# Interleaving k and q heads over partitions, holding engines for the first groups' due steps, and whole Newton products in a fused attention and two-layer FFN kernel

## The chip, the cores and the metric

The kernel runs on one core of one Trainium2 chip. Its measure is the device time of one launch in microseconds, the median of several runs; smaller is better. The program is a single instruction stream per engine: TensorE (PE; its weight loads are listed apart as PEld), VectorE (DVE), ScalarE (ACT), GpSimd (POOL) and SyncE (SP), which issues the transfers.

## The reference, cut to what matters

```python
def _attn_ref(q, k, v):                      # 4 batches, 8 heads, 576 rows, 64 columns
    q_lm, k_lm = means of 18 neighbouring rows      # 32 landmarks per head
    A, Bm, C = sm(q, k_lm), sm(q_lm, k_lm), sm(q_lm, k)
    Z = Bm.transpose(0, 1, 3, 2) / (norm1(Bm) * norminf(Bm) + 1e-06)   # norms over the last two axes
    for _ in range(6):
        Z = 2 * Z - Z @ Bm @ Z
    return A @ Z @ C @ v
x = attention as (2304, 512)
h = x @ w_in;  x = (h * tanh(softplus(h))) @ w_out      # Mish layer, 512 -> 2048 -> 512
h = x @ w_in2; out = (h * sigmoid(h)) @ w_out2          # SiLU layer
```

The weights arrive as float64 and are turned into float32 on the chip. The attention is a Nyström approximation; its inner loop is a Newton iteration for the inverse of one 32x32 matrix per head.

## The kernel before, in words

**Work.** A "group" is four heads of one batch, so that four 32x32 landmark matrices fill 128 partitions; two groups make a batch, eight groups (0 to 7) make the attention. The FFN is split into units of 288 tokens and 128 hidden columns: six `h` matmuls (`h<-at,wp`), the Mish on ACT, a split of the result into a high and a low part (`g`), and twelve `y` matmuls (`y<-g,wo`). Layer 1 has 128 units, so 2304 matmuls of 128x288, which stand in batches' order: a batch needs both its groups, and the product of its matrix `ut` with a block of four decoded `w_in` tiles (`projection`, rows `t<-wa,ut`), from which come the `wp` tiles that the `h` matmuls take as weights. Layer 2 follows as seven-product blocks.

**Order.** The program is put in order while it is built: the class `Line` keeps a clock `now`, the time from which each engine is free, and a table of estimated costs. Every strand of work (a "chain") is a Python generator that yields the engine of its next step; `run` picks, among the chains that are due, the one of lowest rank (table `KINDS`: ranks 0 and 1 hold the FFN's gating, the projections `X` and the first two groups' chains `M` and `F`; ranks 2 and 3 hold the later groups and the decoding of weights). Each engine executes its instructions in the order so written. Where the plan has nothing for PE, it writes products of the identity (`y<-ident`, `h<-ident` and `t<-ident` without a second name), whose results nobody reads.

**Steps named below.** `Group.rows` loads k and q, 32 partitions per head. `transposed` and `scores` make the scores; `sums` makes the landmark sums (`lmk`, `lmq`) on DVE or POOL; in groups 2 and 3 they come from products with the constant `twice` instead. `newton` has six steps. In a step, `each` issues four 32x32 products, one per head (`t<-yu` or `h<-yu`), and DVE forms the next `yu`. The block-diagonal tile `bd` is built once per group on DVE and used for one last product (`bd,yu`). `decode` turns weights into float32: one ACT and three DVE instructions per tile (`wa`, `m`), for `wo` two more.

All engine instructions have line 226 (the helper `issue`), and all transfers line 237. In the changed program these are lines 257 and another; the names of tiles tell instructions apart.

Of the kernel before, what the change touches and what calls it, by code (L numbers as in the profile page):

```python
# [11 lines left out]
FP32 = mybir.dt.float32  # L12
# [47 lines left out]
def width(ap):  # L60
    return ap.size() // ap.shape[0]


class Line:
# [7 lines left out]
    WINDOW, ENOUGH = 4.096 / 1.2, 3060  # L72
    AGAIN = {"V": 0.12, "A": 0.12, "P": 0.1, "T": 0.0}
    FIXED = {"V": 0.07, "A": 0.1, "P": 0.05, "T": 0.0133}
    EACH = {"V": 1.04e-3, "A": 0.82e-3, "P": 2.29e-3, "T": 0.417e-3}

    def __init__(self, nc):
        self.nc = {"V": nc.vector, "A": nc.scalar, "P": nc.gpsimd, "T": nc.tensor}
        self.free = dict.fromkeys(["V", "A", "P", "T", "D", "W"], 0.0)
        self.now = 0.0  # L80
        self.free["D"] = 0.45
        self.end = 0.0
        self.last = set()
# [4 lines left out]
        self.small = False  # L88
        self.count = itertools.count()

    def cost(self, e, name, kw):
        src = kw.get("in_", kw.get("in0"))
        n = width(src if name == "tensor_reduce" else kw["out"])
        psum = src is not None and src.space == bass.MemoryType.PSUM
        more = 0.0
        if e == "T":
            tiled = kw["out"].shape[0] < 96 and "lhsT" in kw
            if tiled and (kw["out"].start_partition() or kw["lhsT"].start_partition()):
                return 0.027 * self.clock()
            n *= self.clock() * self.columns(kw)  # L100
        elif e == "A":
            more = -0.04 if psum else 0.0
            more += 0.14 if "accum_out" in kw else 0.09 if kw.get("func") == ACTF.Ln else 0.0
        elif e == "P" and name == "tensor_scalar":
            n *= 0.46
        elif e == "V" and name in ("copy", "tensor_copy", "tensor_scalar", "scaled"):
# [9 lines left out]
        return self.FIXED[e] + more + n * self.EACH[e]  # L116

    @staticmethod
    def span(ap):
# [71 lines left out]
    def issue(self, engines, name, kw, bias=0.0):  # L191
# [4 lines left out]
        e = min(engines, key=lambda e: start(e) + self.cost(e, name, kw) + (bias if e == "V" else 0.0))  # L196
        at = start(e)
        if e == "T":
            small = kw["out"].shape[0] < 96
            if self.small and not small:  # L200
                at = max(at, self.free["T"] + 0.055)
            self.small = small
        end = at + self.cost(e, name, kw)
# [25 lines left out]
    def transfer(self, engine, **kw):  # L229
        ap = kw["out"] if kw["out"].space == bass.MemoryType.SB else kw["in_"]  # L230
        start = max(self.now, self.free["D"], self.depend("D", "dma", kw))
        self.free["D"] = start + width(ap) * ap.shape[0] * 4 / 0.36e6
        end = self.free["D"] + 2.1
        self.end = max(self.end, end)
        self.last.add("D")
        self.record("D", kw, end)
        return engine.dma_start(**kw)  # L237

    def add(self, chain, rank, engine="W", ready=None):
        self.chains.append([self.now if ready is None else ready, rank, next(self.count), engine, chain])  # L240
        return self.chains[-1]

    def step(self, c):
        self.end = 0.0
        self.last = set()
        engine = next(c[4], "done")
        if engine == "done":
            self.chains.remove(c)
            return
        if not self.end:  # L250
# [10 lines left out]
    def run(self):  # L261
        while True:
            due = [c for c in self.chains if self.start_of(c) <= self.now]
            if not due:
                return
            self.step(min(due, key=lambda c: (KINDS[c[1]][0], c[2])))
# [81 lines left out]
def kernel(  # L348
# [648 lines left out]
    def heads(x, b, e):  # L997
        return x[b].rearrange("(i e) s d -> e i s d", e=GB)[e]

    class Group:  # L1000
# [7 lines left out]

        def load(self):
            kn = self.kn = qkv_p.tile([128, J, D], FP32, tag="kn", name="kn")  # L1010
            rows = [heads(x, self.b, self.hg).rearrange("i (l j) d -> i l (j d)", j=J) for x in (k, q)]
            self.rows(kn, rows[0])
            self.k_at = line.end
            if self.g == 1:
# [46 lines left out]
        def transposed(self, nm, src):  # L1061
# [6 lines left out]
            for j in range(0, J2, 3):  # L1068
# [30 lines left out]
        def main(self):  # L1099
# [28 lines left out]
            VAs.scaled(out=lmT[:, 0, :], in_=pl[0][:, 0, :], scalar1=1.0 / J)  # L1128
            VAs.scaled(out=lmT[:, 1, :], in_=pl[0][:, 1, :], scalar1=scale / J)
            Ring.give(pl)  # L1130
            self.lmT = lmT
            yield "W"
# [4 lines left out]
            for h in range(HG):  # L1137
# [56 lines left out]
            Ring.give(py)  # L1194
            yield "V"

            bd = self.bd = s_p.tile([128, HG, LM], FP32, tag="bd", name="bd")
            V.scalar_tensor_tensor(
                out=bd,
                in0=bn.rearrange("p (o l) -> p o l", o=1).to_broadcast([128, HG, LM]),  # L1200
                scalar=rc,
                in1=mask,
                op0=ALU.mult,
                op1=ALU.mult,
            )
            marks.add((g, "y"))
            yield "T"
            yield from until(marked((g, "u")))
# [3 lines left out]
        def each(out, lhsT, rhs, **kw):  # L1212

            for h in range(HG):
                r = slice(32 * h, 32 * h + 32)
                T.matmul(out=out[r], lhsT=lhsT[r], rhs=rhs[r], start=True, stop=True)

        def newton(self):

            yu, g = self.yu, self.g  # L1220
            for it in range(6):
# [15 lines left out]
            T.matmul(  # L1237
                out=pu[0][r], lhsT=yu[:, LM:], rhs=self.bd.rearrange("p h l -> p (h l)"), start=True, stop=True
            )
            yield "W"  # L1240
            VA.copy(out=ut_t[self.b][r].rearrange("p h l -> p (h l)"), in_=pu[0][r])
# [290 lines left out]
```

## Time and profile before

| | us |
|---|---|
| median of three runs | 858.45 (857.98 to 859.84) |
| span of the profiled execution, first to last instruction | 855.9 |
| PE busy | 824.3 (96%) |
| ACT busy | 450.6 |
| DVE busy | 515.6 |
| POOL busy | 288.1 |

The profile is one execution. The difference of 2.55 us between its span and the median of the runs is what lies around the first and last instruction, and the variation of runs. A float32 product that is not a transpose is listed as two matmul instructions, and a matmul's listed duration overlaps the next one's, so its price is read from start to start.

### The profile page before, as it was taken

The numbers are of one execution on the slowest core, as the hardware profiler recorded it, in microseconds if no ns is written. First come the engines' busy times: TensorE is split into PE (matmuls) and PEld (weight loads), VectorE is DVE, ScalarE is ACT, GpSimd is POOL, SyncE is SP. The second block draws the span as 40 slices with busy tenths as digits, with TensorE's granted clock in tenths as the row PEclk, the third lists the DMA queues.
The fourth block names the chain that finished last, engine by engine and source line by source line (L and its number), as shares of the span: only waits on it lengthen the run. The fifth ranks groups of instructions, "written<-read, shape, count | busy, mean of one in ns | idle before, by whom it ended". The sixth has DMA issues, their size and how long they took to land.

```text
span 855.9 us, 15972 instructions
## 1 busy us (share of the span) xinstructions
PE 824.3 (96%) x6084; PEld 726.1 (85%) x6084; DVE 515.6 (60%) x1030; ACT 450.6 (53%) x997; POOL 288.1 (34%) x331
## 2 busy tenths in 40 slices
PE   7999989899999999999999999999999999999996
PEld 5877767676899989989999898898898898998885
DVE  4976644453586958414516999767555567555542
ACT  5574776667555565433425755544544454544432
POOL 4241524342355555624323434311223221232210
PEclk9999999999999999999999999999999999999999
DMA  9874225200345554241125422101400000200002
GB/s 246 237 224 154 59 55 139 57 29 2 106 148 176 157 197 155 80 129 56 57 79 156 152 99 87 37 1 38 111 1 1 0 1 8 67 1 2 0 1 75
DMA packets 42254, 72.36 MB, mean 85 GB/s; under 512 B 5056, under 2 KB 31680, under 8 KB 42176
## 3 DMA queue, kind: packets, MB, share of 16 engines
q1 hardware_dynamic: 41600, 70.54, 27.1%
q8 instruction: 48, 0.79, 0.4%
q10 hardware_dynamic: 576, 0.79, 0.3%
q14 instruction: 30, 0.25, 0.1%
HBM read 57.15 MB, written 14.16 MB: 83 GB/s over the span
## 4 chain that ended last, share of the span: by engine, by line
PE 86%; ACT 7%; DMA 3%; issue 1%; DVE 1%; SPq 1%; POOL 0%; ACTq 0%; POOLq 0%; DVEq 0%
PE y L226 47%; PE h L226 31%; PE t L226 8%; ACT L226 3%; ACT z L226 1%; DMA wst<-in_moe_w_in_dram 1%; SPq L237 1%; DMA kn<-in_k_dram 1%; ACT g L226 1%; ACT ec L226 1%; DMA wst<-in_moe_w_out_dram 1%; DMA wst<-ys 0%; ACT at L226 0%; DMA out_dram<-ysb 0%; ACT wp L226 0%
## 5 line engine op out<-in xcount | busy, mean ns | idle before, releaser
L226 PE MATMUL y<-g,wo 128*128 128x288 f32 x1536 | 235.0, 301 | 1.4 <-POOL g L226 1.4
L226 PEld LDWEIGHTS y<-g,wo 128*128 128x128 f32 x1536 | 209.8, 188 | 15.3 <-issue 9.8
L226 PE MATMUL y<-wo,xg 128*128 128x512 f32 x693 | 179.8, 394 | 0.0
L226 POOL TENSOR_TENSOR g<-z,g 128x288 fp32r<-128x288 f32 x128 | 114.5, 905 | 174.3 <-ACT g L226 150.5
L226 PEld LDWEIGHTS y<-wo,xg 128*128 128x128 f32 x693 | 128.4, 188 | 20.9
L226 DVE TENSOR_TENSOR z<-h,z 128x384 f32<-128x384 f32 x164 | 89.4, 554 | 70.9 <-PE h L226 68.8
L226 PE MATMUL h<-at,wp 128*128 128x288 f32 x768 | 121.0, 302 | 5.8 <-ACT z L226 5.7
L226 PEld LDWEIGHTS h<-at,wp 128*128 128x128 f32 x768 | 106.3, 188 | 19.1 <-ACT z L226 8.8
L226 ACT ACTIVATE z<-h 128x288 f32<-128x288 f32 x128 | 51.6, 413 | 73.9 <-PE h L226 71.5
L226 ACT ACTIVATE z<-z 128x384 f32<-128x384 f32 x94 | 49.2, 525 | 34.3 <-DVE z L226 34.0
L226 POOL TENSOR_TENSOR wo<-m,wo 128x512 fp32r<-128x512 f32 x32 | 46.5, 1454 | 54.7 <-ACT wo L226 47.7
L226 DVE SCALAR_TENSOR_TENSOR m<-wst,m 128x512 int32<-128x512 int32 x64 | 61.9, 968 | 1.1
L226 PE MATMUL h<-xg,wp 128*128 128x384 f32 x288 | 58.0, 336 | 1.5 <-DVE z L226 1.5
L226 PE MATMUL h<-xg,wf 128*128 128x384 f32 x288 | 57.9, 336 | 0.4 <-DVE z L226 0.4
L226 ACT CAST g<-z 128x288 fp32r<-128x288 f32 x123 | 51.8, 435 | 7.4 <-PE y L226 6.2
L226 PEld LDWEIGHTS h<-xg,wp 128*128 128x128 f32 x288 | 51.3, 188 | 5.0 <-DVE z L226 1.9
L226 PEld LDWEIGHTS h<-xg,wf 128*128 128x128 f32 x288 | 51.2, 188 | 3.9 <-DVE z L226 0.9
L226 DVE TENSOR_TENSOR xg<-z,xg 128x384 fp32r<-128x384 f32 x73 | 41.4, 570 | 20.9 <-ACT xg L226 20.6
L226 POOL TENSOR_TENSOR wf<-m,wf 128x256 fp32r<-128x256 f32 x20 | 16.2, 809 | 96.8 <-ACT wf L226 96.8
L226 PE MATMUL y<-wo,wp 128*128 128x512 f32 x171 | 44.9, 394 | 0.0
L226 ACT ACT_TABLE_LOAD x31 | 39.8, 1283 | 1.7 <-PEq L1516 0.7
L226 DVE TENSOR_TENSOR wp<-t,wp 128x512 fp32r<-128x512 f32 x32 | 20.6, 685 | 30.5 <-ACT wp L226 30.4
(229 smaller groups left out, 1179.8 us busy)
## 6 DMA issues: line engine op xcount, KB each, us to landing
wst<-in_moe_w_out_dram SPq DMA_DIRECT2D x32, 512.0 KB, 5.8
wst<-in_moe_w_in_dram SPq DMA_DIRECT2D x28, 512.0 KB, 5.4
kn<-in_k_dram SPq DMA_DIRECT2D x32, 144.0 KB, 5.3
vn<-in_v_dram SPq DMA_DIRECT2D x8, 576.0 KB, 6.1
yh<-ysb SPq DMA_DIRECT2D x32, 144.0 KB, 1.9
ysb<-yh SPq DMA_DIRECT2D x32, 144.0 KB, 2.9
ys<-ysb SPq DMA_DIRECT2D x32, 144.0 KB, 2.0
qn<-in_q_dram SPq DMA_DIRECT2D x28, 144.0 KB, 3.6
```

The source lines that it names most:

```text
L226: r = getattr(self.nc[e], name)(**kw)
L237: return engine.dma_start(**kw)
```

## The change

Three edits and a new table of estimates. In `rows`, the four heads of k and q are spread over the partitions (partition 4l+h holds landmark l of head h) where each head had 32 neighbours; `transposed` and `main` undo it when they copy from PSUM. In `run`, an engine that a first-group chain or a projection will want within 0.4 us is not given to a chain of rank 2 or 3. In `newton`, groups 2 to 7 multiply by a block-diagonal tile in one product of 128x96, and DVE builds that tile anew for every step (`blocks`); the old `bd` is built after the six steps. The estimates get new numbers: POOL's cost per element, transfer rates, table loads of ACT's functions, and the switch of PE between 32-wide tiles and whole products.

```diff
-    EACH = {"V": 1.04e-3, "A": 0.82e-3, "P": 2.29e-3, "T": 0.417e-3}
+    EACH = {"V": 1.04e-3, "A": 0.82e-3, "P": 2.67e-3, "T": 0.417e-3}
+    TABLES = {ACTF.Exp: "exp", ACTF.Mish: "mish", ACTF.Silu: "silu"}
+    LOAD = 1.3
+    AHEAD = 0.4
...
@@ run @@
             due = [c for c in self.chains if self.start_of(c) <= self.now]
+            soon = {c[3] for c in self.chains if c[1] in "MFX" and not c[5] and self.now < c[0] <= self.now + self.AHEAD}
+            due = [c for c in due if KINDS[c[1]][0] < 2 or c[3] == "W" or c[3] not in soon]
...
@@ Group.load, Group.rows @@
-            rows = [heads(x, self.b, self.hg).rearrange("i (l j) d -> i l (j d)", j=J) for x in (k, q)]
+            rows = [heads(x, self.b, self.hg).rearrange("i (l j) d -> l i (j d)", j=J) for x in (k, q)]
...
-                line.transfer(nc.sync, out=to[32 * i:32 * i + 32].rearrange("p j d -> p (j d)"), in_=of[i])
+                line.transfer(nc.sync, out=to[i::HG].rearrange("l j d -> l (j d)"), in_=of[:, i])
...
@@ transposed @@
-                VA.copy(out=t[:, j:j + 3].rearrange("p j h l -> p j (h l)"), in_=pt[0])
+                VA.copy(out=t[:, j:j + 3], in_=pt[0].rearrange("p j (l h) -> p j h l", h=HG))
...
@@ newton @@
+        def blocks(self, y, by):
+
             V.scalar_tensor_tensor(
+                out=self.bd,
+                in0=y.rearrange("p (o l) -> p o l", o=1).to_broadcast([128, HG, LM]),
+                scalar=by,
                 in1=mask,
                 op0=ALU.mult,
                 op1=ALU.mult,
             )
...
+            whole = g > 1
             for it in range(6):
                 lo = 0 if it < 5 else LM
+                if whole:
+                    yield "V"
+                    self.blocks(yu[:, 0:LM], 1.0)
+                    yield "T"
                 yield from until(self.banks.ready)
                 pn = self.banks.take([128, LM + D], FP32)
-                self.each(pn[0][:, lo:], yu[:, 0:LM], yu[:, lo:])
+                if whole:
+                    T.matmul(out=pn[0][:, lo:], lhsT=bd, rhs=yu[:, lo:], start=True, stop=True)
+                else:
+                    self.each(pn[0][:, lo:], yu[:, 0:LM], yu[:, lo:])
...
+            yield "V"
+            self.blocks(self.bn, self.rc)
+            yield "T"
```

The order on PE around the first projection (`t<-wa,ut`), from the end of group 1's Newton steps (`h<-yu`, `h<-bd,yu`) on, before:

```order
L226 MATMUL h<-bd,yu 64x128
L226 MATMUL y<-ident 128x128 x6
L226 MATMUL t<-Tk,twice 128x128 x9
L226 MATMUL t<-Tq,twice 128x128 x9
L226 MATMUL y<-ident 128x128 x6
L226 MATMUL t<-wa,ut_141 32x512 x8
L226 MATMUL y<-ident 128x128 x14
L226 MATMUL t<-lmT 32x32 x4
L226 MATMUL y<-ident 128x128 x6
L226 MATMUL h<-at_637,wp 128x288 x2
```

and in the change:

```order
L257 MATMUL h<-bd,yu 64x128
L257 MATMUL t<-ident,kn 128x128 x3
L257 MATMUL t<-ident,qn 128x128 x3
L257 MATMUL y<-ident 128x128 x2
L257 MATMUL t<-ident,kn 128x128 x3
L257 MATMUL y<-ident 128x128 x2
L257 MATMUL t<-ident,qn 128x128 x3
L257 MATMUL y<-ident 128x128 x6
L257 MATMUL t<-wa,ut_141 32x512 x8
L257 MATMUL y<-ident 128x128 x20
L257 MATMUL t<-Tk,twice 128x128 x9
L257 MATMUL h<-at_644,wp 128x288 x2
```

The eighteen products with `twice`, which belong to group 2, stood ahead of the projection and now stand behind it, nine of them ahead of the first FFN matmul (`h<-at,wp`).

The order on DVE during group 1's Newton steps (`yu<-yu,h`; those of group 0 read `t`), with the decoding of weights (`wa`, `m`) between them, before:

```order
L226 SCALAR_TENSOR_TENSOR yu<-yu,h 128x96
L226 SCALAR_TENSOR_TENSOR yu<-yu,t 128x64
L226 SCALAR_TENSOR_TENSOR wa<-aw_145,wa 128x512 x2
L226 SCALAR_TENSOR_TENSOR yu<-yu,h 128x96
L226 TENSOR_SCALAR m<-m 128x512
L226 SCALAR_TENSOR_TENSOR wa<-aw_145,wa 128x512
L226 SCALAR_TENSOR_TENSOR m<-wst,m 128x512
L226 SCALAR_TENSOR_TENSOR yu<-yu,h 128x96
L226 TENSOR_SCALAR m<-m 128x512
L226 SCALAR_TENSOR_TENSOR m<-wst,m 128x512
L226 SCALAR_TENSOR_TENSOR yu<-yu,h 128x64
```

and in the change, from the same step of group 0 (`yu<-yu,t 128x64`) on:

```order
L257 SCALAR_TENSOR_TENSOR wa<-wst,wa 128x512
L257 SCALAR_TENSOR_TENSOR bd<-bn,rc,mask 128x128
L257 SCALAR_TENSOR_TENSOR yu<-yu,h 128x96
L257 TENSOR_SCALAR wa<-wa 128x512 x2
L257 SCALAR_TENSOR_TENSOR wa<-wst,wa 128x512
L257 SCALAR_TENSOR_TENSOR yu<-yu,h 128x96
L257 SCALAR_TENSOR_TENSOR wa<-aw_145,wa 128x512
L257 SCALAR_TENSOR_TENSOR wa<-wst,wa 128x512
L257 SCALAR_TENSOR_TENSOR yu<-yu,h 128x64
L257 SCALAR_TENSOR_TENSOR wa<-aw_145,wa 128x512
```

The decoding of `m` tiles has moved behind group 1's last step, and so has part of the decoding of `wa`.

The order on PE in a late group's Newton steps among the FFN's matmuls, before (group 6):

```order
L226 MATMUL t<-yu 32x96 x4
L226 MATMUL y<-g,wo 128x288 x2
L226 MATMUL t<-ident,kn 128x128 x3
L226 MATMUL y<-g,wo 128x288
L226 MATMUL t<-yu 32x96 x4
L226 MATMUL y<-g,wo 128x288 x3
```

and in the change (group 6):

```order
L257 MATMUL t<-yu,bd 128x96
L257 MATMUL y<-g,wo 128x288
L257 MATMUL t<-ident,qn 128x128 x3
L257 MATMUL y<-g,wo 128x288 x3
L257 MATMUL t<-lmT 32x32 x4
L257 MATMUL h<-at_1338,wp 128x288 x6
L257 MATMUL h<-at_2200,wp 128x288 x2
L257 MATMUL t<-yu,bd 128x96
```

Four 32x32 products have become one whole product, and more FFN matmuls stand between two steps. On DVE, group 2's steps read in the change:

```order
L257 SCALAR_TENSOR_TENSOR bd<-yu,mask 128x128
L257 TENSOR_SCALAR lmT<-t 128x128
L257 SCALAR_TENSOR_TENSOR m<-wst,m 128x512
L257 TENSOR_SCALAR m<-m 128x512
L257 SCALAR_TENSOR_TENSOR yu<-yu,t 128x96
L257 TENSOR_REDUCE nmb<-t 128x1
L257 SCALAR_TENSOR_TENSOR m<-wst,m 128x512
L257 SCALAR_TENSOR_TENSOR bd<-yu,mask 128x128
```

where there was a `yu` row alone; the `bd` rows are new, 36 in all.

## Rows read from the trace of the kernel before

**Rows 1.** Windows by stage: length, busy us per engine, granted clock, DMA share, GB/s.

```profile
0.00:50.50 50.50, 45.63 (x576) 36.19 (x577) 38.30 (x102) 26.84 (x67) 18.54 (x31) 1.00 0.91 251
...
83.10:223.70 140.60, 130.23 (x1452) 99.32 (x1451) 66.32 (x200) 97.74 (x201) 52.09 (x61) 1.00 0.21 57
```

**Rows 2.** PE's longest waits from 83.1 to 223.7 us: total, times, longest.

```profile
PE t L226 <- ACT ec L226: 5.8, 5, 1.5
PE h L226 <- ACT z L226: 3.0, 4, 1.0
```

**Rows 3.** PE's timeline once the attention is over: start, length, instruction, count.

```profile
223.68 6.75 PE L226 MATMUL y<-g,wo 128*128 128x288 f32 x48
230.27 4.20 PE L226 MATMUL h<-at,wp 128*128 128x288 f32 x30
```

**Rows 4.** PE's timeline in group 7's Newton steps.

```profile
214.75 0.37 PE L226 MATMUL t<-yu 32*32 32x96 f32 x8
215.05 1.06 PE L226 MATMUL y<-g,wo 128*128 128x288 f32 x6
216.04 0.37 PE L226 MATMUL t<-yu 32*32 32x96 f32 x8
```

**Rows 5.** PE's timeline: group 0's first k, group 1's first q.

```profile
5.65 0.87 PE L226 MATMUL t<-ident,kn 128*128 128x128 f32 x3 [1.47 <-DMA kn<-in_k_dram]
...
13.20 0.52 PE L226 MATMUL h<-ident,wp 128*128 128x128 f32 x3 [0.79 <-DMA wp<-in_q_dram]
```

**Rows 6.** Windows while k and q load, and while weights load.

```profile
3.00:13.00 10.00, 7.10 (x37) 5.75 (x35) 4.51 (x4) 3.25 (x7) 3.36 (x5) 1.00 1.03 231
...
48.00:54.00 6.00, 6.00 (x70) 4.79 (x62) 3.77 (x15) 4.80 (x10) 2.31 (x2) 1.00 1.02 409
```

**Rows 7.** SP's timeline: the issues of the first load.

```profile
0.74 1.78 SPq L237 DMA_DIRECT2D kn<-in_k_dram  x4
```

**Rows 8.** Timelines: group 1's `lmq` on POOL (first, last), its `lmk` on DVE.

```profile
13.22 1.41 POOL L226 TENSOR_TENSOR t<-wp 128x576 f32<-128x576 f32 x1 [1.29 <-DMA wp<-in_q_dram]
...
16.45 0.45 POOL L226 TENSOR_TENSOR lmq<-t,t 128x128 f32<-128x128 f32 x1
...
10.78 2.17 DVE L226 TENSOR_REDUCE lmk<-kn 128x64 f32<-128x1152 f32 x1 [2.79 <-DMA kn<-in_k_dram]
```

**Rows 9.** DVE's timeline: a decode instruction between group 1's Newton steps.

```profile
38.36 0.68 DVE L226 SCALAR_TENSOR_TENSOR wa<-aw,wa 128x512 int32<-128x512 int32 x1
```

**Rows 10.** PE's timeline from group 1's last product to the first FFN matmul.

```profile
41.15 0.43 PE L226 MATMUL h<-bd,yu 128*64 128x128 f32 x2
...
42.22 2.17 PE L226 MATMUL t<-Tk,twice 128*128 128x128 f32 x18
...
46.24 0.82 PE L226 MATMUL y<-ident 128*128 128x128 f32 x6
46.99 1.09 PE L226 MATMUL t<-wa,ut 64*32 64x512 f32 x16
...
50.52 0.51 PE L226 MATMUL h<-at,wp 128*128 128x288 f32 x2
```

**Rows 11.** PE's timeline around the second projection.

```profile
71.66 0.60 PE L226 MATMUL h<-ident 128*128 128x128 f32 x4
...
78.42 1.85 PE L226 MATMUL t<-wa,ut 64*32 64x512 f32 x16
...
83.11 0.50 PE L226 MATMUL h<-at,wp 128*128 128x288 f32 x2
```

**Rows 12.** All `bd` builds on DVE: min/median/max ns, first and last start.

```profile
L226 DVE SCALAR_TENSOR_TENSOR bd<-bn,rc,mask x8: 338/385/1240, 26.3 to 205.6; 128x128 f32<-128x128 f32 x8
```

**Rows 13.** Timelines of DVE and POOL at the longest `bd` build.

```profile
31.02 1.24 DVE L226 SCALAR_TENSOR_TENSOR bd<-bn,rc,mask 128x128 f32<-128x128 f32 x1
...
30.70 1.41 POOL L226 TENSOR_TENSOR at<-at,ar 128x576 f32<-128x576 f32 x1 [4.83 <-DVE ar L226]
```

**Rows 14.** The page's group of ACT's table loads: busy us, mean ns, idle before.

```profile
L226 ACT ACT_TABLE_LOAD x31 | 39.8, 1283 | 1.7 <-PEq L1516 0.7
```

More of the change, by code (lines that the diff above doesn't have):

```diff
@@ L74 @@
     FIXED = {"V": 0.07, "A": 0.1, "P": 0.05, "T": 0.0133}
-    EACH = {"V": 1.04e-3, "A": 0.82e-3, "P": 2.29e-3, "T": 0.417e-3}
+    EACH = {"V": 1.04e-3, "A": 0.82e-3, "P": 2.67e-3, "T": 0.417e-3}
+    TABLES = {ACTF.Exp: "exp", ACTF.Mish: "mish", ACTF.Silu: "silu"}
+    LOAD = 1.3
+    AHEAD = 0.4
+    TO_TILES, FROM_TILES, WEIGHTS = 0.092, 0.273, 0.107
     def __init__(self, nc):
@@ L88, in __init__ @@
         self.small = False
+        self.table = "exp"
         self.count = itertools.count()
@@ L96, in cost @@
         if e == "T":
-            tiled = kw["out"].shape[0] < 96 and "lhsT" in kw
-            if tiled and (kw["out"].start_partition() or kw["lhsT"].start_partition()):
-                return 0.027 * self.clock()
+            if "lhsT" not in kw:
+                return 0.002 + n * 2 * self.clock() * self.EACH["T"]
+            if kw["out"].shape[0] < 96:
+                at_once = 128 // kw["out"].shape[0] * (2 if kw["lhsT"].shape[0] == 64 else 1)
+                if kw["lhsT"].shape[0] == 128:
+                    at_once = 1
+                first = 0.0 if self.small else max(0.0, self.WEIGHTS - n * 2 * self.EACH["T"])
+                return first + n * 4 * self.clock() * self.EACH["T"] / at_once
+            if n == 512:
+                more = 0.005
+            if self.columns(kw) == 4:
+                n = max(n, 64)
             n *= self.clock() * self.columns(kw)
@@ L102, in cost @@
             more = -0.04 if psum else 0.0
-            more += 0.14 if "accum_out" in kw else 0.09 if kw.get("func") == ACTF.Ln else 0.0
+            more += 0.1 if "accum_out" in kw else 0.0
+            if name == "scaled":
+                more += 0.1
+            if src is not None and not psum and abs(src.ap[-1][0]) == 2:
+                more += 0.045
+            if self.table_of(name, kw) not in (None, self.table):
+                more += self.LOAD
         elif e == "P" and name == "tensor_scalar":
             n *= 0.46
+        elif e == "P" and "in1" in kw and not kw["in1"].ap[-1][0]:
+            n *= 0.73
         elif e == "V" and name in ("copy", "tensor_copy", "tensor_scalar", "scaled"):
@@ L116, in cost, with table_of @@
         return self.FIXED[e] + more + n * self.EACH[e]
+    def table_of(self, name, kw):
+        return self.TABLES.get(kw.get("func")) if name == "activation" else None
     @staticmethod
@@ L198, in issue @@
         if e == "T":
-            small = kw["out"].shape[0] < 96
+            small = kw["out"].shape[0] < 96 and "lhsT" in kw
             if self.small and not small:
-                at = max(at, self.free["T"] + 0.055)
+                at = max(at, self.free["T"] + self.FROM_TILES)
+            elif small and not self.small:
+                at = max(at, self.free["T"] + self.TO_TILES)
+        end = at + self.cost(e, name, kw)
+        if e == "T":
             self.small = small
-        end = at + self.cost(e, name, kw)
+        elif e == "A":
+            self.table = self.table_of(name, kw) or self.table
         if e == "T":
@@ L231, in transfer @@
         start = max(self.now, self.free["D"], self.depend("D", "dma", kw))
-        self.free["D"] = start + width(ap) * ap.shape[0] * 4 / 0.36e6
+        rate = 0.3e6 if ap.shape[0] == 96 else 0.4e6
+        self.free["D"] = start + width(ap) * ap.shape[0] * 4 / rate
         end = self.free["D"] + 2.1
@@ L239, in add @@
     def add(self, chain, rank, engine="W", ready=None):
-        self.chains.append([self.now if ready is None else ready, rank, next(self.count), engine, chain])
+        self.chains.append([self.now if ready is None else ready, rank, next(self.count), engine, chain, False])
         return self.chains[-1]
@@ L249, in step @@
             return
+        c[5] = not self.end
         if not self.end:
@@ L1127, in main @@
             lmT = s_p.tile([128, 2, 128], FP32, tag="lmT", name="lmT")
-            VAs.scaled(out=lmT[:, 0, :], in_=pl[0][:, 0, :], scalar1=1.0 / J)
-            VAs.scaled(out=lmT[:, 1, :], in_=pl[0][:, 1, :], scalar1=scale / J)
+            order = "p (h l) -> p h l" if g in SUMMED else "p (l h) -> p h l"
+            for i, by in enumerate((1.0 / J, scale / J)):
+                VAs.scaled(
+                    out=lmT[:, i, :].rearrange("p (h l) -> p h l", h=HG),
+                    in_=pl[0][:, i, :].rearrange(order, h=HG),
+                    scalar1=by,
+                )
             Ring.give(pl)
@@ L1195, in main @@
             yield "V"
[L1197 to L1205, printed above, removed]
+            self.bd = s_p.tile([128, HG, LM], FP32, tag="bd", name="bd")
             marks.add((g, "y"))
@@ L1237, in newton @@
             T.matmul(
-                out=pu[0][r], lhsT=yu[:, LM:], rhs=self.bd.rearrange("p h l -> p (h l)"), start=True, stop=True
+                out=pu[0][r], lhsT=yu[:, LM:], rhs=bd, start=True, stop=True
             )
```

6 lines of the change are left out of this document (added).

## Prediction

> **What bounds the kernel now.** I read the windows by stage first, then PE's waits, then PE's timeline at single places. PE is busy for 130.2 of 140.6 us while the later groups run beside the FFN, and ACT for 97.7, DVE for 66.3, POOL for 52.1 [rows 1]. PE's waits in that stage end on ACT, in the two largest groups 5.8 and 3.0 us, so about 9 us, or 6% [rows 2]. So from 83 us on PE's own work sets the pace, and an instruction taken off PE there is worth its full price, less those 6%. After the attention, 48 FFN matmuls take 230.27 - 223.68 = 6.59 us, 0.137 each [rows 3]. The first 50.5 us are another matter: PE looks busy for 45.6 of them [rows 1], but much of that is products of the identity that nobody reads. There the end is set by the chain from the landing of group 1's q to the first projection and the first FFN matmul at 50.52 us [rows 5, 10].
>
> So two things can shorten the span: an earlier first FFN matmul, if what follows moves with it, and less work on PE between 83 and 224 us.
>
> **The start, part by part.**
>
> Load. Group 0's first k is ready at 5.65 us, group 1's first q at 13.20, three loads later: 2.52 us per load of 4 x 144 KB [rows 5]. The core then moves 231 GB/s with its DMA engines full, against 409 when weights fill all 128 partitions [rows 6]. A load of 590 KB at 409 GB/s would take 1.44 us, but SP needs 1.78 us to issue its four transfers [rows 7], so the first load lands 1.1 us earlier and each further one 0.74: 3.3 us. No row shows a strided destination, so the ends are 0 (the rate is not the partitions' doing) and 4 x 1.08 = 4.3; I take 3.3, since 32 or 128 partitions is what sets the two windows apart.
>
> [...]
>
> Group 1's `lmq`. On POOL it runs from 13.22 to 16.90 us; a DVE reduction of the same size takes 2.17 [rows 8]. DVE has the `lmk` to do first, so of the 1.3 us about 0.6 are left; ends 0 and 1.3. On POOL nothing is queued behind it.
>
> Newton steps of group 1. By the order, the decode instructions between the last three steps are five of 0.68 us and two of 0.42 before, three and two in the change; an instruction of 0.68 stands in the row [rows 9]. With one or two more ahead of these, 1.5 us; ends 0 and 3.
>
> `twice`. From group 1's last product at 41.15 us to the projection at 46.99 pass 5.84 us, of which 4.02 are the eighteen products with `twice` [rows 10]. They go. What is late next is the decoding that was put off: seven DVE rows, four of them 0.68, one `bd` of 0.34 [rows 12] and two shorter, less their overlap 3.4 us from the last step, some 3.3 from the last product with the hand-over. Gain 2.5, ends 1 and 4. Nine `twice` products now stand between projection and first FFN matmul, which took 3.53 us [rows 10]; I charge 1 us, at most 2.0.
>
> Sum: 3.3 + 0.6 + 1.5 + 2.5 - 1 = 7 us, between -1 and 12.6. The first FFN matmul would start near 43.5 us.
>
> Then the FFN runs out of `wp` after 72 matmuls, before as in the change: PE idles with identity products from 71.66 us, the second projection starts at 78.42, the FFN goes on at 83.11 [rows 11]. That projection stands 31.4 us behind the first one. It waits for four decoded tiles, which ACT and DVE handle between Mish, table loads and group 2's chain; their transfers run from 48 to 54 us [rows 6], long before. By the order these instructions stand in the same places relative to the first projection, so I keep the 31.4 us and the 7 us carry over.
>
> **Newton on PE.** Six FFN matmuls and one step of four 32x32 products repeat every 216.04 - 214.75 = 1.29 us [rows 4]; six matmuls at 0.137 are 0.82, so a step costs 0.47, though only 0.30 pass from its start to the next matmul's. The rest is lost at the change between tiles and whole products. A whole float32 product of 128 columns takes 4.02 / 18 = 0.22 us [rows 10]. With 96 columns that would be 0.17 if columns alone counted (lower end); the upper end is 0.43, the listed length of `bd,yu` [rows 10]. I take 0.22, because a single product also loads its own weights. Outside the idle stretches stand 31 steps before (one of group 2, thirty of groups 3 to 7) and 33 in the change, as fewer of group 2's fall into the pause: 31 x 0.47 = 14.6 against 33 x 0.22 = 7.3. Less the 6% of waits this saves 7 us; with 0.17 it is 9, with 0.43 nothing.
>
> [...]
>
> **What is added elsewhere.** 36 `bd` builds on DVE, 0.34 to 1.24 us [rows 12], are 12 us or more; DVE is idle for 74 of 140.6 us in that stage [rows 1], so the time is covered. They lengthen each Newton step, so attention ends later in the FFN: the first projections of batches 1, 2 and 3 stand behind 234, 516 and 760 FFN matmuls (before 212, 436, 594), and the batches begin at 288, 576, 864. The margins are 54, 60 and 104 matmuls, 7.4 to 14 us at 0.137; nothing is charged. The copies that undo the interleaving read with a stride; ACT is idle for 43 us of the stage, so nothing again, though a copy twice as long would show in the waits on ACT. ACT has 27 table loads where it had 31, 5.1 us at 1.28 [rows 14]; this could shorten the waits on ACT by up to that, and I count none. SP issues its transfers as before but for one `w_in` tile that goes ahead of group 3's k. The second layer's instructions stay, so its time stays.
>
> **The sum.** 7 + 7 = 14 us. The profiled span of 855.9 us becomes 841.9; with the 2.5 us that the median has above it, 844.4. I forecast 844.
>
> **Rivals.**
>
> A. One of the two savings doesn't arrive. Either the second projection is tied to something else than the first (all seven microseconds go into a longer pause at 72 matmuls; for it: ACT is the busy engine there), or a single whole product costs near 0.43 us. 858.45 - 7 = 851.
>
> B. Neither arrives: the loads stay at 231 GB/s, the decoding that was put off eats what `twice` gave up, and whole products cost as much as tiles. 858. Against it: two unrelated places must fail.
>
> C. Slower. Each whole product waits in PE's queue for a `bd` that DVE builds one step earlier, and behind it wait the FFN matmuls. The place is the 36 builds. POOL works 37% of that stage [rows 1], and a `bd` that met a POOL instruction took 1.24 us in place of 0.34 and ended when that had ended [rows 13]: 0.9 us. With 24 of 36 so caught, 21.6 us against the 14 saved: 866. It decides from 16 on (16 x 0.9 = 14.4). For it: a decode instruction ahead of the `bd` on DVE adds another 0.68. Against it: between two steps stand mostly ten FFN matmuls or more, 1.4 us, and a `bd` and a `yu` need 0.6.
>
> D. More: the start gains its upper end, whole products cost 0.17 and fewer table loads shorten ACT's waits: 858.45 - 12.6 - 9 - 5 = 832 at most.
>
> **How the numbers follow.** Forecast (838 to 850) 0.50, A 0.23, B 0.07, C 0.12, D (under 838) 0.08. A measurement of this kernel tells about 0.2% (1.7 us) from no change. Faster by more: 0.50 + 0.23 + 0.08 = 0.81; within: 0.07; slower: 0.12. The range 833 to 857 holds the forecast, A and most of D, and leaves out C and most of B, some 0.2.
>
> **What would show it.** Right, if group 1's first q is transposed near 10 us and the window over the loads shows over 300 GB/s; if the first FFN matmul starts near 43.5 us and the second projection 31 us after the first; if a whole product adds about 0.22 us between FFN matmuls; and if the stage after the attention keeps 0.137 us per matmul. Wrong, if PE waits on DVE's `bd` ahead of these products, if the pause at 72 matmuls grows by as much as the start shrank, or if PE's waits on ACT exceed 9 us.

## The result, and the profile after

| us | median of the runs | first FFN matmul | behind 74 FFN matmuls | from there to 800 | from 800 to the end |
|---|---|---|---|---|---|
| before | 858.42 | 50.5 | 83.9 | 167.7 | 604.3 |
| change | 848.38 (846.67 to 850.29) | 50.9 | 84.3 | 157.7 | 604.9 |

The change is faster: ratio 0.988, interval 0.987 to 0.990, 10.0 us, where 14 were forecast. The profiled span is 846.9 us in place of 855.9. The columns behind the median are starts of FFN matmuls in the two traces; 74 is just behind the pause, in which the FFN has no `wp` left after 72 matmuls and PE writes products of the identity; by the 800th the attention is all but over. I call these two the marks. The start gained nothing, and the whole gain lies between the marks.

Windows of before over that stretch (length, busy us of PE, PEld, DVE, ACT, POOL, clock, DMA share, GB/s):

```profile
83.90:251.60 167.70, 157.33 (x1664) 125.57 (x1664) 85.65 (x223) 113.24 (x237) 66.17 (x75) 1.00 0.26 76
```

Windows of the change over the start (beside [rows 1]), the same stretch, the load, and three short ones:

```profile
0.00:50.95 50.95, 40.59 (x525) 30.87 (x525) 36.85 (x101) 25.68 (x62) 12.67 (x25) 0.97 0.75 234
...
84.30:242.00 157.70, 151.13 (x1480) 130.25 (x1479) 89.48 (x257) 101.05 (x220) 59.32 (x71) 0.98 0.19 56
...
3.00:8.00 5.00, 2.61 (x18) 2.03 (x17) 2.33 (x2) 0.96 (x2) 0.11 (x1) 1.00 0.74 230
...
11.60:15.00 3.40, 3.12 (x16) 2.75 (x15) 3.09 (x3) 1.80 (x5) 0.00 (x0) 0.50 0.94 238
...
90.10:93.50 3.40, 3.40 (x17) 3.40 (x16) 0.36 (x4) 2.28 (x7) 1.56 (x2) 0.50 0.00 0
107.10:110.60 3.50, 2.97 (x14) 2.95 (x15) 1.16 (x6) 1.60 (x4) 1.16 (x1) 0.51 0.00 0
```

PE is busy for 6.2 us less and idle for 6.6 us in place of 10.4. In the three short stretches its clock is halved (0.50, 0.50 and 0.51); in the trace of before the clock is full (1.00) from 11 to 853 us. The loads still move 230 GB/s, but now at a DMA share of 0.74, where [rows 6] had 1.03.

PE's longest waits in that stretch of the change, beside [rows 2]:

```profile
PE h L257 <- ACT z L257: 2.5, 4, 0.8
PE t L257 <- DVE yu L257: 1.9, 2, 1.2
PE t L257 <- ACT ec L257: 1.4, 2, 0.8
```

SP's timeline of the change, the first two loads, beside [rows 7]:

```profile
0.74 2.46 SPq L269 DMA_DIRECT2D kn<-in_k_dram  x4
3.24 2.50 SPq L269 DMA_DIRECT2D qn<-in_q_dram  x4
```

PE's timeline of the change, beside [rows 5, 10, 11], and whole products of late groups beside [rows 4]:

```profile
5.31 0.52 PE L257 MATMUL t<-ident,kn 128*128 128x128 f32 x3 [1.13 <-DMA kn<-in_k_dram]
...
12.95 0.87 PE L257 MATMUL h<-ident,wp 128*128 128x128 f32 x3 [0.28 <-DMA wp<-in_q_dram]
...
41.30 0.40 PE L257 MATMUL h<-bd,yu 128*64 128x128 f32 x2 [0.95 <-DVE bd L257]
...
45.37 1.47 PE L257 MATMUL t<-wa,ut 64*32 64x512 f32 x16 [0.87 <-ACT Tk L257]
46.77 2.40 PE L257 MATMUL y<-ident 128*128 128x128 f32 x20
49.01 2.18 PE L257 MATMUL t<-Tk,twice 128*128 128x128 f32 x18
50.95 0.51 PE L257 MATMUL h<-at,wp 128*128 128x288 f32 x2
...
78.86 1.09 PE L257 MATMUL t<-wa,ut 64*32 64x512 f32 x16
...
197.33 0.35 PE L257 MATMUL t<-yu,bd 128*128 128x96 f32 x2
197.47 0.77 PE L257 MATMUL h<-at,wp 128*128 128x288 f32 x4
...
221.99 0.36 PE L257 MATMUL t<-yu,bd 128*128 128x96 f32 x2
222.13 1.31 PE L257 MATMUL h<-at,wp 128*128 128x288 f32 x8
223.28 0.95 PE L257 MATMUL y<-g,wo 128*128 128x288 f32 x6
224.07 0.35 PE L257 MATMUL t<-yu,bd 128*128 128x96 f32 x2
```

One load takes SP 2.5 us, and group 1's first q comes three of those behind the first k (12.95 - 5.31 = 3 x 2.55). That SP now sets this pace shows in the time from a transfer's issue to its landing. For group 1's q, the last of the four loads, its median (the last number) is 5.1 us in before, where SP starts a load every 1.85 us and one is ready every 2.52, and 2.6 in the change, as for the first loads, where it starts one every 2.53 and one is ready every 2.55:

```profile
wp<-in_q_dram SPq DMA_DIRECT2D x4, 144.0 KB, 5.1
```

```profile
wp<-in_q_dram SPq DMA_DIRECT2D x4, 144.0 KB, 2.6
```

The first projection stands 1.6 us earlier than before, the second one 33.5 us behind it in place of 31.4. A whole product is followed by the next FFN matmul after 0.14 us, and from one whole product over fourteen FFN matmuls to the next pass 224.07 - 221.99 = 2.08 us.

SP's longer issues also put off what SP issues behind the loads. A decode instruction of ACT waits 1.82 us for its weights, `ec` stands behind it in ACT's queue, and PE waits 1.36 us for `ec`. ACT's timeline of the change, then PE's:

```profile
20.90 0.66 ACT L257 ACTIVATE wa<-wst 128x512 f32<-128x512 f32 x1 [1.82 <-DMA wst<-in_moe_w_in_dram]
```

```profile
22.31 0.44 PE L257 MATMUL y<-ident 128*128 128x128 f32 x2 [1.36 <-ACT ec L257]
```

Behind the 800th matmul PE's largest wait in the change is a new one, 2.6 us. PE's timeline there, then ACT's:

```profile
330.17 1.35 PE L257 MATMUL h<-at,wp 128*128 128x288 f32 x8 [2.61 <-ACT z L257]
```

```profile
326.03 0.41 ACT L257 ACTIVATE z<-h 128x288 f32<-128x288 f32 x1 [0.23 <-PE h L257]
328.82 0.66 ACT L257 ACTIVATE wi<-wst 128x512 f32<-128x512 f32 x1 [2.38 <-DMA wst<-in_moe_w_in_dram]
329.39 0.42 ACT L257 CAST g<-z 128x288 fp32r<-128x288 f32 x1
329.71 0.41 ACT L257 ACTIVATE z<-h 128x288 f32<-128x288 f32 x1
```

A decode instruction waits 2.38 us for its weights, and the Mish behind it in ACT's queue, for which PE waits 2.61 us, has to wait too.

### The profile page after: what moved, and what is told of

It is laid out like the page before. It is cut to its first block, busy times and chain, and to the rows that moved or that the text cites. A ratio compares the mean times of both kernels' runs of the same rounds, so it can differ in the third digit from the quotient of the medians.

```text
span 846.9 us, 15538 instructions
## 1 busy us (share of the span) xinstructions
PE 815.8 (96%) x5866; PEld 729.2 (86%) x5866; DVE 523.8 (62%) x1082; ACT 446.2 (53%) x983; POOL 277.2 (33%) x322
## 4 chain that ended last, share of the span: by engine, by line
PE 86%; DVE 5%; DMA 3%; ACT 2%; SPq 2%; issue 2%; POOL 0%; ACTq 0%; DVEq 0%; POOLq 0%
PE y L257 48%; PE h L257 30%; PE t L257 8%; SPq L269 2%; DMA wst<-in_moe_w_in_dram 1%; DVE m L257 1%; DMA out_dram<-ysb 1%; ACT z L257 1%; DVE bd L257 1%; DVE wa L257 0%; DVE z L257 0%; DVE wp L257 0%; ACT wp L257 0%; DVE yu L257 0%; ACT g L257 0%
## 5 line engine op out<-in xcount | busy, mean ns | idle before, releaser
L257 PEld LDWEIGHTS y<-g,wo 128*128 128x128 f32 x1536 | 211.1, 190 | 13.3 <-issue 10.9
L257 DVE TENSOR_TENSOR z<-h,z 128x384 f32<-128x384 f32 x161 | 87.9, 555 | 70.2 <-PE h L257 68.3
L257 POOL TENSOR_TENSOR wo<-m,wo 128x512 fp32r<-128x512 f32 x31 | 44.7, 1444 | 53.5 <-ACT wo L257 48.4
L257 DVE SCALAR_TENSOR_TENSOR m<-wst,m 128x512 int32<-128x512 int32 x64 | 55.2, 870 | 0.4
L257 PEld LDWEIGHTS h<-xg,wf 128*128 128x128 f32 x288 | 51.2, 188 | 3.9 <-ACT z L257 0.9
L257 PEld LDWEIGHTS h<-xg,wp 128*128 128x128 f32 x288 | 51.2, 188 | 3.7 <-DVE z L257 0.6
L257 ACT CAST g<-z 128x288 fp32r<-128x288 f32 x118 | 49.5, 436 | 7.9 <-PE y L257 6.5
L257 POOL TENSOR_TENSOR wf<-m,wf 128x256 fp32r<-128x256 f32 x17 | 12.6, 742 | 83.9 <-ACT wf L257 83.9
L257 ACT CAST xg<-z 128x384 fp32r<-128x384 f32 x74 | 38.0, 513 | 1.6
L257 PEld LDWEIGHTS y<-wo,wp 128*128 128x128 f32 x171 | 31.7, 188 | 5.2
```

The costliest lines, as they stand in the source:

```text
L257: r = getattr(self.nc[e], name)(**kw)
```

## The experiments

All times are medians, all ratios against the kernel before, whose runs beside these had medians of 858.2 to 858.6 us. The columns are as above; they are of the one profiled execution, which took 2.1 us more than the median in d_estimates, 3.1 less in e_one_block, and lies between these in the others.

| kernel | us | ratio, interval | first FFN matmul | behind 74 | 74 to 800 | 800 to end |
|---|---|---|---|---|---|---|
| c_tiled | 846.12 | 0.986 (0.984 to 0.988) | 49.9 | 81.1 | 160.2 | 603.1 |
| c_block | 847.60 | 0.987 (0.984 to 0.989) | 49.6 | 83.0 | 154.8 | 608.0 |
| c_no_hold | 857.70 | 0.999 (0.997 to 1.000) | 56.5 | 84.1 | 165.6 | 606.9 |
| c_two_queues | 847.36 | 0.986 (0.984 to 0.988) | 50.4 | 83.7 | 154.9 | 607.2 |
| d_one_issue | 845.44 | 0.984 (0.982 to 0.986) | 46.2 | 79.5 | 157.8 | 606.5 |
| d_estimates | 851.47 | 0.991 (0.990 to 0.993) | 57.0 | 87.9 | 159.6 | 604.3 |
| d_hold | 864.52 | 1.007 (1.006 to 1.009) | 53.4 | 91.0 | 165.4 | 608.2 |
| d_old_estimates | 871.70 | 1.015 (1.013 to 1.018) | 50.2 | 88.1 | 167.2 | 615.4 |
| e_one_from3 | 837.04 | 0.975 (0.973 to 0.976) | 47.4 | 78.6 | 154.7 | 601.6 |
| e_one_tiled | 843.40 | 0.982 (0.981 to 0.984) | 47.7 | 78.9 | 160.0 | 602.3 |
| e_one_block | 877.11 | 1.021 (1.019 to 1.023) | 69.6 | 102.9 | 162.8 | 606.5 |
| e_whole | 865.80 | 1.008 (1.006 to 1.010) | 51.2 | 84.0 | 166.0 | 612.5 |

My first theory was that of the prediction with its start taken out: the whole products are the gain. The rivals were the hold, and the interleaved rows.

**c_tiled.** The change with tiles in every step.

```diff
-            whole = g > 1
+            whole = False
```

> The changed kernel, but all groups' Newton steps as four 32x32 products again (the interleaving, the hold and the new estimates stay). Theory 1, the gain of 10 us is PE time saved by whole products: 36 steps at about 0.25 us more each, so about 857 to 860 us, and the first FFN matmul at 51 us as in the change. Theory 2, the gain comes from the new order (hold and estimates) and the products' price is hidden: 850 us or less.

It was not slower, 846.1, and theory 1 fell. What the whole products take off PE is there: against c_block, whose order is that of the change and whose clock was full between the marks, the tiles add 4.0 us in the 33 steps themselves and 3.2 us in the FFN matmuls, 7.2 in all or 0.22 per step. Most of the 3.2 us stands just ahead of a step: from start to start such an FFN matmul takes 0.23 us in c_tiled, and 0.14 in c_block ahead of a whole product. But with tiles PE's idle time there is 3.7 us in place of 6.6, and the FFN goes on 1.9 us earlier than in c_block, 3.2 earlier than in the change. PE's timeline of c_tiled:

```profile
215.51 0.37 PE L257 MATMUL t<-yu 32*32 32x96 f32 x8
215.81 1.06 PE L257 MATMUL h<-at,wp 128*128 128x288 f32 x6
216.80 0.31 PE L257 MATMUL t<-yu 32*32 32x64 f32 x8
```

Six matmuls and a step take 1.29 us, as in [rows 4]; in the change four matmuls follow a whole product after 0.14 us.

**c_block.** The change with contiguous rows, as before, and the copies from PSUM that belong to them.

```diff
-                line.transfer(nc.sync, out=to[i::HG].rearrange("l j d -> l (j d)"), in_=of[:, i])
+                line.transfer(nc.sync, out=to[32 * i:32 * i + 32].rearrange("p j d -> p (j d)"), in_=of[i])
```

> The changed kernel with each head's k and q in 32 neighbouring partitions again. Theory 1, SP's issue of a strided transfer (0.64 us against 0.46) has become the limit of the first loads, so that the interleaving gains nothing there: issues 0.46 us apart, group 1's first q transposed at about 13 us as in both kernels, total within 2 us of 848.4. Theory 3, spreading shortens the loads' path: 3 us slower than 848.4, and the first q later than in the change.

With four transfers per load the interleaving makes no difference that the medians show (0.8 us, within the spread of either). At the start it costs: c_block's first FFN matmul comes 1.3 us earlier. SP issues the first `w_in` weights at 9.72 us in place of 12.03, ACT doesn't wait for them, and PE doesn't wait for `ec`. ACT's timeline of c_block:

```profile
19.23 0.68 ACT L257 ACTIVATE wa<-wst 128x512 f32<-128x512 f32 x1
```

The order on PE is that of the change, row for row, and the stretch from 74 to 800 takes 154.8 us in place of 157.7, with no half clock in it: so the two half-clock stretches cost the change 2.9 us there. c_block had its own elsewhere, of 6.8 us each from 8.0 and from 325.4 us on.

**c_no_hold.** The change without the hold.

```diff
-            due = [c for c in due if KINDS[c[1]][0] < 2 or c[3] == "W" or c[3] not in soon]
```

> The changed kernel without the hold of engines for the first groups' due steps. Theory 1 (whole products are the gain): within 2 us of 848.4. Theory 2 (order is the gain): 5 us or more slower, with the eighteen products of the constant ahead of the first projection again and the first FFN matmul after 53 us.

Almost all of the gain is gone, but not where the hold is meant to act: the first projection is 6 us later, with the eighteen `twice` products ahead of it as theory 2 had it, yet the second comes at 78.69 us, where the change has it at 78.86. PE's timeline of c_no_hold shows the loss:

```profile
129.77 0.38 PE L257 MATMUL y<-ident 128*128 128x128 f32 x2
...
130.97 1.10 PE L257 MATMUL h<-ident 128*128 128x128 f32 x8
...
137.17 0.60 PE L257 MATMUL y<-ident 128*128 128x128 f32 x4
137.70 1.09 PE L257 MATMUL t<-wa,ut 64*32 64x512 f32 x16
138.72 2.19 PE L257 MATMUL y<-ident 128*128 128x128 f32 x18
```

Batch 1's first projection stands behind 288 FFN matmuls, where the change has it behind 234. At 288 the FFN has no `wp` left, and PE spends some 7 us on products of the identity. The margin of 54 matmuls that I had charged at nothing is what the hold buys.

**c_two_queues.** The change with q of groups 0 and 1 issued by ACT.

```diff
-                line.transfer(nc.sync, out=to[i::HG].rearrange("l j d -> l (j d)"), in_=of[:, i])
+                line.transfer(by, out=to[i::HG].rearrange("l j d -> l (j d)"), in_=of[:, i])
```

Here `by` is ACT's queue for these q and SP's for all else.

> The changed kernel with the q of the first two groups issued from ACT's queue, k from SP's. Theory 1 (the loads wait for SP's issues): two queues issue in parallel, group 1's first q is transposed before 10.5 us in place of 12.95, and the total is 1 to 4 us below 848.4 as far as the order on PE and DVE lets it through. If the DMA engines are the limit: first q near 13 us and no change.

The test did not tell the theories apart. Both queues issue from the start; the window of c_two_queues, then ACT's timeline:

```profile
3.00:8.00 5.00, 1.73 (x9) 1.35 (x8) 0.56 (x1) 0.00 (x0) 0.30 (x1) 1.00 0.88 304
```

```profile
0.73 2.77 ACTq L269 DMA_DIRECT2D qn<-in_q_dram  x4
3.89 4.14 ACTq L269 DMA_DIRECT2D wp<-in_q_dram  x4
```

At first the loads move 304 GB/s in place of 230, from 8 to 13 us 241, and a transfer lands 4.2 to 4.4 us after its issue in place of 2.6. Since k and q now load side by side, the first k was transposed at 7.45 us in place of 5.31. Group 1's first q was transposed at 14.55, behind other transposes and not behind its load: PE was not idle ahead of it. So a second queue does raise the rate of the first loads, but not to the 399 GB/s of the next run; why not is not shown.

So whole products were not the gain, and the hold could not be told from the order that it makes. My second theory, "theory 1" in the expectations that follow, was that the gain is the order of ACT's and DVE's work, which the estimates set, and that the early start was lost to SP's issues.

**d_one_issue.** The change with one transfer per load.

```diff
-            for i in range(HG):
-                line.transfer(nc.sync, out=to[i::HG].rearrange("l j d -> l (j d)"), in_=of[:, i])
+            line.transfer(nc.sync, out=to.rearrange("p j d -> p (j d)"), in_=of)
```

> The changed kernel, with each load of k or q as one transfer over all 128 partitions in place of four over every fourth partition; the instructions on the other engines keep their order. Theory 1 (SP's issues of 0.64 us set the pace of the first loads): group 1's first q is transposed at 10 to 11 us in place of 12.95, group 0's scores start near 15 in place of 16.87, and the first FFN matmul, the second projection and the end come some 2 us earlier: 846. Rival (the memory gives no more than 230 GB/s to these loads, however they are issued): 12.95 again and 848.4. Second rival (one transfer keeps fewer of the DMA engines busy): the first k later than 5.31 and 850.

Theory 1 held, with more than it expected at the start. Windows of d_one_issue, then its PE:

```profile
3.00:8.00 5.00, 4.22 (x19) 3.42 (x17) 2.90 (x2) 0.96 (x2) 1.50 (x2) 1.00 1.00 399
```

```profile
4.96 0.90 PE L257 MATMUL t<-ident,kn 128*128 128x128 f32 x3 [0.77 <-DMA kn<-in_k_dram]
...
10.77 0.49 PE L257 MATMUL h<-ident,wp 128*128 128x128 f32 x3
```

399 GB/s with all engines busy, and 1.66 us per load by the landings (first k 4.91 us, group 1's q 9.90). Both projections and the FFN come 4.7 us earlier, in the same order and at the same distances. At the end 2.9 us of it are left by the medians, 3.1 by the spans; the rest is lost behind the 800th matmul.

**d_estimates.** The kernel before with the new numbers of `cost`, `place` and `transfer` alone (diff above, all but `run`, `rows` and `newton`).

```diff
+            if self.table_of(name, kw) not in (None, self.table):
+                more += self.LOAD
...
+                at = max(at, self.free["T"] + self.FROM_TILES)
```

> The kernel before with the planner's new estimates alone: no hold, four tiles in each Newton step, contiguous rows. By the order, 32 idle products stand at the 72nd FFN matmul in place of 42, and the projection of batch 1 stands behind 194 and 214 FFN matmuls. Theory 1 (most of the gain is the order of ACT's and DVE's instructions beside the FFN, which the estimates set; the hold is needed only where whole products lengthen the chain): PE's waits on ACT fall from 10 to some 4 us between FFN matmuls 74 and 800, 849 to 852. Rival (the hold makes the gain): 857 to 859.

7 us, with nothing else changed. PE's waits from 87.9 to 247.5 us in d_estimates:

```profile
PE t L257 <- ACT ec L257: 1.8, 5, 0.8
PE h L257 <- ACT z L257: 1.5, 2, 1.1
```

The 8.8 us of these two in before [rows 2] are now 3.3, and PE's idle time between the marks falls from 10.4 to 4.0 us.

**d_hold.** The kernel before with the hold alone.

```diff
+            due = [c for c in due if KINDS[c[1]][0] < 2 or c[3] == "W" or c[3] not in soon]
```

> The kernel before with the hold alone, old estimates: by the order, 58 idle products at the 72nd FFN matmul in place of 42, and 14 more near the 300th. Theory 1 (hold and estimates only help together): PE's waits on ACT stay near 10 us and the longer pause costs 1 to 3 us, 858 to 861. Rival (the hold by itself makes the gain): 848 to 851.

Slower by 6 us, more than expected: the second projection comes at 86.48 us, and PE is idle for 11.4 us between the marks.

**d_old_estimates.** The change with the old `cost`, `place` and `transfer`.

```diff
-                at = max(at, self.free["T"] + self.FROM_TILES)
+                at = max(at, self.free["T"] + 0.055)
```

> The changed kernel with the old estimates: whole products, hold and interleaving stay. By the order, 68 idle products at the 72nd FFN matmul in place of 44 and 18 at the 156th. Theory 1 (the order that the estimates set makes most of the gain, whole products some 4 us of it): 852 to 856. Rival (whole products and the hold make the gain whatever the estimates are): 848 to 850.

Slower than theory 1 had it, by 23 us against the change. PE is idle for 14.3 us between the marks, and 10.5 us are lost behind them.

**e_whole.** The kernel before with `newton` and `blocks` of the change, nothing else.

```diff
-                self.each(pn[0][:, lo:], yu[:, 0:LM], yu[:, lo:])
+                    T.matmul(out=pn[0][:, lo:], lhsT=bd, rhs=yu[:, lo:], start=True, stop=True)
```

> The kernel before with whole products from group 2 on alone: old estimates, no hold. By the order, 48 idle products at the 72nd FFN matmul and 54 between the 138th and the 156th, which before has not. Theory 1 (whole products take some 7 us off PE, but with the old estimates the order leaves PE idle for more than that): 858 to 866. Rival (whole products gain by themselves): 850 to 853.

7.4 us slower: PE spends some 7 us on identity products between the 74th and the 300th matmul, all at the 138th and the 156th as the order had it, and waits for 12.8 us between the marks. Alone, the edit that takes work off PE loses.

**e_one_from3.** d_one_issue with whole products from group 3 on.

```diff
-            whole = g > 1
+            whole = g > 2
```

> The changed kernel with one transfer per load and whole products from group 3 on alone, so that group 2's Newton steps are tiles again; by the order 28 idle products stand at the 72nd FFN matmul in place of 44. Theory 1 (whole products in group 2 put off the second projection by some 2 us, and gain nothing there because they lie in the pause; the rest of the gain stays): the 74th FFN matmul at 76 to 77 us in place of 79.5, and 838 to 842. Rival (what is won in the pause is lost to the order that the planner makes of the later groups, whose clock and waits decide): 845 or above.

837.0 us, the fastest of all, 8.4 below d_one_issue. Of theory 1 only the total came nearly true, 1 us below its range: the 74th matmul comes 0.9 us earlier, not 3. Another 3.1 us lie between the marks, where the clock is full (1.00, d_one_issue 0.98), and 4.9 behind them; of these, 2.8 are waits between the 1150th and the 1500th matmul, 0.5 us here and 3.3 there, above all the one on `z` shown for the change. PE's waits in e_one_from3 from 76 to 255 us, and its windows between and behind the marks:

```profile
PE h L257 <- ACT z L257: 2.4, 4, 1.2
PE t L257 <- ACT ec L257: 0.8, 1, 0.8
```

```profile
78.60:233.30 154.70, 150.59 (x1522) 128.47 (x1521) 99.36 (x277) 100.09 (x207) 58.57 (x70) 1.00 0.21 62
233.30:835.00 601.70, 589.53 (x3506) 539.73 (x3504) 375.85 (x659) 295.90 (x657) 194.18 (x217) 1.00 0.23 74
```

**e_one_tiled.** d_one_issue with tiles in every step (`whole = False`).

> The changed kernel with one transfer per load and four tiles in every Newton step. With four transfers per load the tiles gave 846.1 beside 848.4. Theory 1 (the earlier loads carry over in full, 4.7 us at the first FFN matmul, whatever the steps are): 841 to 843. Rival (loads that arrive early gain 3 us, as with whole products): 843 to 844.

2.7 us below c_tiled, as the rival had it: the first FFN matmul comes 2.2 us earlier than there, not 4.7. It is 6.4 us above e_one_from3. Between these two, which share group 2's tiles, whole products gain: 160.0 - 154.7 = 5.3 us between the marks, at full clock in both.

**e_one_block.** c_block with one transfer per load.

```diff
-                line.transfer(nc.sync, out=to[32 * i:32 * i + 32].rearrange("p j d -> p (j d)"), in_=of[i])
...
+            line.transfer(nc.sync, out=to.rearrange("p j d -> p (j d)"), in_=of)
```

> The changed kernel with contiguous rows as before and one transfer per load; the order is that of the changed kernel. Theory 1 (four issues and 32 partitions per transfer made the loads slow, not the place of the rows): a load takes 1.7 to 1.9 us as with interleaved rows, first FFN matmul near 46, 845. Rival (rows of 32 neighbouring partitions in turn are slow in themselves): 2.5 us per load as before, first FFN matmul near 50, 848.

Neither theory. Windows of e_one_block:

```profile
3.00:8.00 5.00, 1.18 (x6) 0.78 (x4) 0.00 (x0) 0.00 (x0) 0.00 (x0) 1.00 0.25 97
```

A quarter of the DMA share, a quarter of the rate, and group 0's first k at 9.60 us. In c_block the same rows, loaded in four transfers, moved 233 GB/s at a share of 1.03 from 3 to 8 us. The slowest loop of this transfer's source runs over 4 heads, that of d_one_issue over 32 landmarks; whether that sets the share is not shown. So this run does not tell what contiguous rows cost by themselves.

## Why the prediction was right, and where not

It had the sign and nearly the size, but 14 = 7 + 7 is not where the 10 us are from. That 848.4 came so near 844 is luck for the most part: the first 7 did not arrive, the second did on PE but was lost again to waits, the clock and a longer pause, and the new estimates, which the sum had at nothing, gained 7 to 23 us. Of the signs that were named, the price of a whole product held; the 300 GB/s, the first FFN matmul near 43.5 us and the distance of 31 us did not.

**The load (3.3 us): a step that failed.** "SP needs 1.78 us to issue its four transfers" was read from transfers into 32 neighbouring partitions [rows 7]. With a destination that steps over four partitions each issue takes 0.62 us, the load 2.5, and SP became the limit just where the DMA engines had been: 0.25 us gained, not 3.3. Behind that the late weights cost PE a wait of 1.4 us (above), which the sum did not have. That spread rows load faster was right for one transfer over all partitions: 399 GB/s in d_one_issue, against 231 of neighbouring rows in before.

**Group 1's `lmq`, its Newton steps, `twice`.** Group 0's scores start at 16.87 us, 2.0 later than before: on PE the `lmk` of group 0 now stands behind six more transposes of q and k, which run at half clock (11.6 to 15.0 us, above). Group 1's last product is only 0.15 later [rows 10]: `lmq` and the Newton steps gained 1.8 of the 2.1 forecast, net of the wait of 1.4 us on `ec` and of 0.95 us in which PE waits for group 1's own `bd` (41.30 us, above). That `bd` is now built behind the six steps, on the way to the first projection. From there to the first projection pass 4.07 us in place of 5.84, 1.8 gained of 2.5. From the projection to the first FFN matmul pass 5.58 in place of 3.53, 2.05 lost where I charged 1. The start's sum is -2.0 + 1.8 + 1.8 - 2.05 = -0.4 us, where I had 7, within the bounds given.

**"I keep the 31.4 us and the 7 us carry over."** The distance is the order's, not a constant: 33.5 us in the change, c_block, c_two_queues, d_one_issue and e_one_block, which share one order, whether the first projection comes at 40.6 us or at 64.0; 32.3 in c_tiled, 27.3 in c_no_hold, 38.2 in d_hold. With an unchanged order an early start carries over to the second projection in full. Rival A's first form, a longer pause, holds for the change by 2.1 us.

**Newton on PE (7 us).** Right, in price and in size. Where at least two FFN matmuls stand on either side and PE doesn't wait, each of them counted at 0.133 us (their median among others of their kind), a step of tiles costs 0.48 us in c_tiled, the mean of 20 places: 0.28 itself, 0.09 in the matmul ahead of it and 0.10 in the one behind. A whole product costs 0.22 in c_block, the mean of 22 places: 0.14 itself and 0.08 behind it. These are, to 0.01, the 0.47 and 0.22 that were worked out; in the rows of the change, 2.08 - 14 x 0.133 is 0.22 too. Over the stretch this made 7.2 us between c_tiled and c_block. So a step of four tiles costs about twice a whole product here (0.48 against 0.22). But the change did not keep the gain: against c_tiled it ended 2.3 us slower, with 2.9 us more of waits, 2.9 us at half clock, and 3.2 us at the end of the pause. e_one_from3 keeps most of it.

**"What is added elsewhere" costs nothing: half wrong.** Between the marks the `bd` builds on DVE did stay covered: 285 ns in the median, 7 of the 36 new ones over 0.6 us where rival C decides from 16 on, and a single wait of PE, 0.68 us at 105.7 us, that ends as one of them does; rival C did not come. But a longer Newton step puts off the projections, and the order decides whether a margin is left: in the change it held (234 of 288), in c_no_hold it did not (288 of 288). In e_whole it held too, at 216; its pauses at the 138th and 156th matmul have another cause, which I did not trace.

**What I left at nothing made the gain.** I left the table loads uncounted ("I count none") and never asked what the new estimates save in PE's waits on ACT. Eight of these kernels are all the combinations of estimates, hold and whole products, and the new estimates gain in each of the four pairs: 7 us alone, 18 with the hold (d_hold, c_tiled), 8 with whole products (e_whole, c_no_hold), 23 with both. PE's waits on ACT between the marks are 10.3 to 13.3 us in the four with old estimates, 1.8 to 4.6 in the four with new ones. It is not the number of table loads: d_hold has 23, before 31, e_one_from3 31 as well. But the estimates set more than the order, since the planner gives an instruction to the engine that it expects to finish first: d_estimates has, table loads aside, 32 instructions fewer on ACT than before and 38 more on DVE over the whole run. No run keeps the engines and changes the order alone. The parts do not add up. Whole products cost 6 to 7 us under three orders (e_whole against before, d_old_estimates against d_hold, c_no_hold against d_estimates), 2 under the fourth (the change against c_tiled), and gain 6 when group 2 is left out (e_one_from3 against e_one_tiled). The hold costs 6 us with the old estimates (before, e_whole) and gains 5 to 9 with the new ones. In some of these comparisons the interleaving differs too, which c_block showed to be worth under 1 us in the median, under one order only.

Four things stay open: which of the new estimates matters; whether they gain by the order or by the choice of engines; where the rest of the 4.9 us that e_one_from3 wins behind the 800th matmul is from; and what sets the clock back, since it fell in the change and in d_one_issue at the same places of one order, but not there in c_block. In the change it fell behind waits of 0.83 and 0.64 us at 87 to 90 us, and 0.68 and 1.21 at 105 to 108.

## What to carry to other kernels

Where a program's order comes from a planner, an edit of one step is also a new order, and its worth can be read only with that order: whole products cost 7 us or gain 6. Price the issue of a transfer with the layout that it will have, and read SP's time and the DMA share together: 230 GB/s at a share of 0.74, each transfer landing 2.6 us after its issue, is another limit than 231 at 1.03 with 5.1 us to the landing of the last load. A margin in a queue of work is worth nothing until it is used up, and then all of it: look at how many matmuls are left when a late step needs them.

## What the runs showed of the hardware

A transfer into 32 partitions with a step of four takes SP 0.62 us to issue, into 32 neighbouring ones 0.45; one into all 128 partitions took 0.59 to 0.64 in d_one_issue, as much as one of the former. Four transfers into neighbouring partitions moved 231 GB/s with all DMA engines busy, those into every fourth partition the same at three quarters of the share, one over all partitions 399 in d_one_issue. With the heads as its slowest loop, one over all partitions moved 97 in e_one_block, at a quarter of the share. Among 128x288 matmuls a Newton step of four 32x32 products cost PE 0.48 us, of which 0.09 fall to the matmul ahead of it and 0.10 to the one behind; one whole product with a block-diagonal tile cost 0.22.
